# Moving v's casts, loads and border copies in a sparse-attention and MoE kernel

## The chip, the cores and the metric

The kernel runs on one core of one Trainium2 chip. The metric is the time of one execution in microseconds (us). Three runs of the kernel before gave 247.07, 248.79 and 249.06; the median is 248.79.

## What is computed

Four batches, eight heads, 768 tokens, head width 64. Each token attends to the tokens less than 16 away and to 24 block summaries: for every block of 32 tokens the maximum of k and the mean of v. The result, 768 x 512 for each batch, goes through one of eight experts, which is chosen from the mean over the batch's tokens.

```python
k_sum = k.reshape(B, H, nb, block, D).max(axis=3)      # block 32
v_sum = v.reshape(B, H, nb, block, D).mean(axis=3)
mask_l = np.abs(pos[:, None] - pos[None, :]) < window  # window 16
scores_s = scale * einsum(q, k_sum) + np.log(block)
a = softmax(concatenate([where(mask_l, scores_l, -1e9), scores_s]))
attn = a @ concatenate([v, v_sum])
e = argmax(mean_over_tokens(x) @ w_gate)               # one expert for a batch
out = gate * (relu(x @ w1[e]) @ w2[e])
```

## The kernel before, in words

**Attention.** Two heads (a pair) are handled at once, in 12 query blocks of 64. A query block sees 96 keys (its 64 and a border of 16 on either side) and the 24 block summaries, 120 rows in all. The steps of a pair, each a Python function that issues its instructions:

- T (line 190): TensorE transposes k (L194), a copy lays it out in windows as kT (L208 on ScalarE in batch 0, L210 on VectorE later), q likewise (L214, L220), VectorE takes the block maxima kmx (L224), GpSimd copies these behind the windows of kT (L230) and clears kT's spare columns (L233).
- QK (line 238), for one half of the query blocks: scores (L245), exponential on ScalarE (L254), mask on VectorE (L256).
- AV (line 267): attention times v (L278), division (L286, L287).
- X (line 295): transposes to the layout of the MoE (L299, L304), with the sums that the gate needs.

**v.** load_v (line 95) brings one batch's v, eight loads on the SP queue, to v_f in fp32. cast_v (L153; L151 on ScalarE) writes it as bf16 into vblk, of which there are two for alternating batches. halo_v (L157, L158) copies the 16 border rows of each query block from its neighbours, by two DMAs inside SBUF. vsum (line 160) forms the block sums on TensorE (L166, 24 matmuls for each batch), copies them out (L174) and broadcasts them into rows 96 to 119 of vblk, by two DMAs on SP (L178). AV reads vblk after all of these.

**MoE.** gate (line 337) finds the expert, and GpSimd issues the loads of its weights (L362, L367), 4 MB in fp32 that arrive as bf16. h (L396, eviction L403 on ScalarE) and o (L410, L418) are the two layers; they write to three PSUM buffers, the tile hps, in turn. vsum and gate take theirs from the same three.

**Order.** The order of the work on each engine is the order in which the Python code issues it; every engine and every DMA queue works its list off in order. Batch 0's attention runs alone, the beginning of batch 1's too (the first LEAD = 14 of its 30 steps). From then on the MoE of batch b runs with the rest of the attention of b+1 and the beginning of b+2's between its groups; the last batch's MoE runs alone. The steps of batch b also prepare v of batch b+1: four casts on GpSimd, two heads each; in halo, first the loads of v for batch b+2, then the border copies; in vs, the sums. q and k are loaded from the GpSimd queue (L90), two heads at a time for batch 0, all of them at the start, and four at a time for later batches. SP also carries the output stores (L419).

Of the kernel before, what the change touches and what calls it, by code (L numbers as in the profile page):

```python
# [22 lines left out]
def kernel(  # L23
# [36 lines left out]
    kt_pool = ctx.enter_context(tc.tile_pool(name="kt", bufs=3))  # L60
    at_pool = ctx.enter_context(tc.tile_pool(name="at", bufs=3))
    xs_pool = ctx.enter_context(tc.tile_pool(name="xs", bufs=3))
# [14 lines left out]
    vblks = [  # L77
        const_pool.tile([128, NJ + 2, H, D + 1], BF16, name=f"vblk{i}") for i in range(2)
    ]
    kps = kps_pool.tile([128, G, SP + 4], BF16, name="kps")  # L80
    qk_nat = {}
# [13 lines left out]
    def load_v(b):  # L95
        for h in range(H):
            nc.sync.dma_start(
                v_f[16:80, :, h, :], v[b, h].rearrange("(j p) d -> p j d", p=QB)
            )

    load_qk(0, 0, 2)
    load_v(0)
    wg_sb = const_pool.tile([128, NDT, E], FP32, name="wg_sb")
# [4 lines left out]
    nc.scalar.activation(warm, warm, ACT.Exp)  # L108

    for pr in range(1, NP):  # L110
        load_qk(0, 2 * pr, 2 * pr + 2)

    identb = const_pool.tile([128, 128], BF16, name="identb")
    make_identity(nc, identb)

    nc.vector.memset(kps.rearrange("p g c -> p (g c)").bitcast(FP32), 0.0)
    nc.vector.memset(v_f[0:16], 0.0)
    for vb in vblks:
        nc.vector.memset(vb[0:KW, 0, :, :], 0.0)
        nc.vector.memset(vb[0:KW, NJ + 1, :, :], 0.0)  # L120
        nc.vector.memset(vb[0:KW, 1 : NJ + 1, :, D : D + 1], 1.0)

    ones_row = const_pool.tile([1, 128], FP32, name="ones_row")
    nc.vector.memset(ones_row, 1.0)

    mask = const_pool.tile([NR, G, QB // G], BF16, name="mask")
    bind = const_pool.tile([80, NJ, 32], BF16, name="bind")
    it_u = const_pool.tile([KW, G, QB // G], I32, name="it_u")
    m2 = const_pool.tile([KW, G, QB // G], BF16, name="m2")
    nc.gpsimd.iota(it_u, pattern=[[-1, G], [-G, QB // G]], base=0, channel_multiplier=1)  # L130
    nc.vector.tensor_scalar(out=mask[0:KW], in0=it_u, scalar1=1, scalar2=None, op0=ALU.is_ge)
    nc.vector.tensor_scalar(out=m2, in0=it_u, scalar1=31, scalar2=None, op0=ALU.is_le)
    nc.vector.tensor_tensor(out=mask[0:KW], in0=mask[0:KW], in1=m2, op=ALU.mult)
    nc.vector.memset(mask[KW:NR], 1.0)

    it_b = const_pool.tile([80, NJ, 32], I32, name="it_b")
    it_p = const_pool.tile([80, NJ, 32], I32, name="it_p")
    b2 = const_pool.tile([80, NJ, 32], BF16, name="b2")
    nc.gpsimd.iota(it_b, pattern=[[QB, NJ], [-BLK, 32]], base=-16, channel_multiplier=1)
    nc.gpsimd.iota(it_p, pattern=[[0, NJ], [0, 32]], base=0, channel_multiplier=1)  # L140
    nc.vector.tensor_scalar(out=bind, in0=it_b, scalar1=0, scalar2=None, op0=ALU.is_ge)
    nc.vector.tensor_scalar(out=b2, in0=it_b, scalar1=BLK - 1, scalar2=None, op0=ALU.is_le)
    nc.vector.tensor_tensor(out=bind, in0=bind, in1=b2, op=ALU.mult)
    nc.vector.tensor_scalar(out=b2, in0=it_p, scalar1=16, scalar2=None, op0=ALU.is_ge)
    nc.vector.tensor_tensor(out=bind, in0=bind, in1=b2, op=ALU.mult)

    def cast_v(b, h0, h1, eng):
        dst = vblks[b % 2][0:80, 1 : NJ + 1, h0:h1, 0:D]
        src = v_f[:, :, h0:h1, :]
        if eng is nc.scalar:  # L150
            nc.scalar.activation(dst, src, ACT.Copy)  # L151
        else:
            eng.tensor_copy(dst, src)  # L153

    def halo_v(b, h0, h1):
        vb = vblks[b % 2]
        nc.sync.dma_start(vb[0:16, 1 : NJ + 1, h0:h1, :], vb[64:80, 0:NJ, h0:h1, :])  # L157
        nc.sync.dma_start(vb[80:96, 1 : NJ + 1, h0:h1, :], vb[16:32, 2 : NJ + 2, h0:h1, :])  # L158

    def vsum(b):  # L160
        vb = vblks[b % 2]
        vs_ps = mps_pool.tile([128, 512], FP32, name="hps", tag="mps")
        HW = H // 2
        for j in range(NJ):
            for hg in range(2):
                nc.tensor.matmul(  # L166
                    vs_ps[32 * hg : 32 * hg + 32, 0 : HW * (D + 1)],
                    lhsT=bind[:, j, :],
                    rhs=vb[0:80, 1 + j, hg * HW : (hg + 1) * HW, :],
                    start=(j == 0),  # L170
                    stop=(j == NJ - 1),
                )
        vsb = sm_pool.tile([64, HW, D + 1], BF16, name="vsb")
        nc.vector.tensor_copy(  # L174
            vsb, vs_ps[0:64, 0 : HW * (D + 1)].rearrange("p (h c) -> p h c", c=D + 1)
        )
        for hg in range(2):
            nc.sync.dma_start(  # L178
                vb[KW:NR, 1 : NJ + 1, hg * HW : (hg + 1) * HW, :],
                vsb[32 * hg : 32 * hg + NB].unsqueeze(1).to_broadcast([NB, NJ, HW, D + 1]),  # L180
            )

    def attn_steps(b):
# [6 lines left out]
        def T(pr):  # L190
            def f():
                for g in range(G):
                    for hh in range(2):
# [4 lines left out]
                        )  # L198
                kT = kt_pool.tile([128, NJ, 128], BF16, name="kT")
                full = kps[:, :, :]  # L200
# [11 lines left out]
                for g in range(G):  # L212
# [16 lines left out]
                )  # L229
                nc.gpsimd.tensor_copy(  # L230
                    kT[:, :, KW:NR], kmx.unsqueeze(1).to_broadcast([128, NJ, NB])
                )
                nc.gpsimd.memset(kT[:, :, NR:128], 0.0)  # L233
                qTs[pr], kTs[pr] = qT, kT
# [3 lines left out]
        def QK(pr, hf):  # L238
            def f():
                sc = sc_pool.tile([128, 2, 512], FP32, name="sc")  # L240
                for jj in range(NH):
                    j = hf * NH + jj
                    for hh in range(2):
                        rs = slice(hh * D, (hh + 1) * D)
                        nc.tensor.matmul(  # L245
                            sc[:, hh, jj * QB : (jj + 1) * QB],
                            lhsT=kTs[pr][rs, j, :],
                            rhs=qTs[pr][rs, j, :],
                            start=True,
                            stop=True,  # L250
                            tile_position=(hh * D, 0),
                        )
                aT = at_pool.tile([128, 2, NH * QB], BF16, name="aT")
                nc.scalar.activation(aT, sc[:, :, 0 : NH * QB], ACT.Exp, scale=SCALE)  # L254
                a3 = aT[0:NR].rearrange("p h (j c) -> p (h j) c", c=QB)
                nc.vector.tensor_tensor(  # L256
                    out=a3,
                    in0=a3,
                    in1=mask.rearrange("p g e -> p (g e)")
                    .unsqueeze(1)  # L260
                    .to_broadcast([NR, 2 * NH, QB]),
                    op=ALU.mult,
                )
                aTs[pr, hf] = aT
            return f

        def AV(pr, hf):
            def f():
                aT = aTs.pop((pr, hf))
                NS = NH // 2  # L270
                ops_raw = ops_pool.tile([128, 512], FP32, name="ops")
                ops = ops_raw[:, 0 : 2 * NS * (D + 1)].rearrange(
                    "p (h s c) -> p h s c", h=2, c=D + 1
                )
                for hh in range(2):
                    for jj in range(NH):
# [3 lines left out]
                            lhsT=aT[0:NR, hh, jj * QB : (jj + 1) * QB],  # L280
                            rhs=vb[0:NR, 1 + j, 2 * pr + hh, :],
                            start=True,
# [31 lines left out]
        def cast(h0):  # L314
            def f():
                if nxt < B:
                    cast_v(nxt, h0, h0 + 2, nc.gpsimd)
            return f

        def halo():  # L320
            if nxt < B:
                if nxt + 1 < B:
                    load_v(nxt + 1)
                halo_v(nxt, 0, H)

        def vs():
            if nxt < B:
                vsum(nxt)

        steps = [  # L330
            T(0), QK(0, 0), T(1), QK(0, 1), AV(0, 0), QK(1, 0), AV(0, 1), T(2),
            QK(1, 1), AV(1, 0), cast(0), X(0), QK(2, 0), AV(1, 1), cast(2), T(3), QK(2, 1), AV(2, 0),
            cast(4), X(1), QK(3, 0), AV(2, 1), cast(6), QK(3, 1), halo, AV(3, 0), X(2), vs, AV(3, 1), X(3),
        ]
        return steps, xT, pooled
# [93 lines left out]

    cast_v(0, 0, 4, nc.vector)  # L430
    cast_v(0, 4, 8, nc.scalar)
    halo_v(0, 0, H)
    load_v(1)
    steps0, xT0, pooled0 = attn_steps(0)
    steps0[0]()
    vsum(0)
    load_qk(1, 0, 4)
    for s in steps0[1:]:
        s()
    moe = moe_groups(0, xT0, *gate(0, pooled0))  # L440
    load_qk(1, 4, 8)

    LEAD = 14
    queue = []
# [14 lines left out]
    pend = []  # L459
    load_qk(2, 0, 4)  # L460
    load_qk(2, 4, 8)
    start_attn(1)
# [43 lines left out]
```

## Time and profile before

| what | us |
|---|---|
| median of three runs | 248.79 |
| the profiled execution, its own time | 248.07 |
| its span, first to last instruction | 246.4 |
| busy: TensorE / VectorE / ScalarE / GpSimd | 154.6 / 99.3 / 92.8 / 50.6 |
| SP's eight loads of batch 0's v, first issue to last | 0.86 to 15.96 |
| border copies of batch 1, 2, 3: first issue | 60.43, 107.84, 156.06 |
| sums of batch 0, 1, 2, 3: first matmul | 26.82, 66.34, 115.30, 160.12 |
| weight loads of the four batches: first issue | 74.40, 124.12, 168.95, 209.62 |
| first MoE matmul; first of the last batch | 97.39; 218.72 |

In a row of the timeline stand the start, the duration, the engine, the line, the operation, what it writes and reads, how many instructions are merged, and in brackets how long the engine had been idle and who released it. In a row of the waits stand the total, how often, and the longest. In a row of a window stand its length, the busy time (and number of instructions) of TensorE, its weight loads, VectorE, ScalarE and GpSimd, the granted clock of TensorE, the DMA engines' busy share and GB/s. In the slices each digit is the busy share of a fortieth of the span, in tenths.

### The profile page before, as it was taken

Reading aid. Unit: us, or ns where it says so; the run is one execution under the profiler, and the core shown is the slowest. Engines: PE = TensorE matmul, PEld = TensorE weight load, DVE = VectorE, ACT = ScalarE, POOL = GpSimd, SP = SyncE. Lnnn points to the kernel's source line nnn. Section 1 sums busy time; section 2 is a strip of 40 time slices with the busy share of each in tenths; the row PEclk is TensorE's granted clock in tenths of the full one; section 3 lists DMA queues with packets and bytes.
Section 4 is the critical chain, followed back from the end, with each engine's and each line's share of the span. In section 5 each row is a group of like instructions: output and inputs, shape, how many; then the busy total and the mean of one; then the engine's idle time right before and its main releaser. Section 6 shows DMA issues by size and latency. Waiting matters only on the chain. (4 is left out here: it accounts for less than half of the span.)

```text
span 246.4 us, 4656 instructions
## 1 busy us (share of the span) xinstructions
PE 154.6 (63%) x1939; PEld 92.9 (38%) x1960; DVE 99.3 (40%) x192; ACT 92.8 (38%) x167; POOL 50.6 (21%) x82
## 2 busy tenths in 40 slices
PE   0200610764252427997779999587699995449993
PEld 0200510653132325654335565243366542125541
DVE  6851040587034547842247883215683542000000
ACT  2006130454120214484415668321467745115532
POOL 7300210055009215320071235003110100200000
PEclk9999999999999999999979999997999999558998
DMA  6993999047717999693479990534990032792033
GB/s 111 205 194 35 145 177 138 8 87 131 109 49 115 189 204 206 144 145 52 94 139 199 242 223 13 119 105 97 182 212 3 1 130 85 115 225 48 0 128 128
DMA packets 45013, 30.38 MB, mean 123 GB/s; under 512 B 26688, under 2 KB 40256, under 8 KB 44864
## 3 DMA queue, kind: packets, MB, share of 16 engines
q0 software_dynamic: 13264, 14.68, 37.3%
q1 hardware_dynamic: 31728, 15.40, 30.3%
q8 instruction: 15, 0.25, 0.4%
q14 instruction: 6, 0.05, 0.1%
HBM read 35.67 MB, written 6.29 MB: 170 GB/s over the span
## 5 line engine op out<-in xcount | busy, mean ns | idle before, releaser
L396 PE MATMUL hps<-xT_b,w_sb 128*128 128x256 bf16 (+1 forms) x246 | 49.4, 343 | 7.4 <-DMA w_sb<-in_moe_w_dram 6.6
L410 PE MATMUL hps<-w_sb,hT_sb 128*128 128x512 bf16 x181 | 46.8, 403 | 1.3 <-issue 1.0
L254 ACT ACTIVATE aT<-sc 128x768 bf16<-128x768 f32 x32 | 25.9, 808 | 42.8 <-PE sc L245 42.8
L403 ACT ACTIVATE hT_sb<-hps 128x512 bf16<-128x512 f32 x64 | 29.9, 491 | 25.9 <-PE hps L396 25.6
L256 DVE TENSOR_TENSOR aT<-aT,mask 120x768 bf16<-120x768 bf16 x32 | 23.6, 736 | 36.4 <-ACT aT L254 36.4
L418 ACT ACTIVATE o_sb<-hps,gcol 128x512 f32<-128x512 f32 x24 | 16.5, 687 | 43.4 <-PE hps L410 32.6
L396 PEld LDWEIGHTS <-w_sb 128*128 128x128 bf16 x256 | 24.0, 102 | 23.2 <-DMA w_sb<-in_moe_w_dram 7.5
L230 POOL COPY kT<-kmx 128x288 bf16<-128x288 bf16 x16 | 9.2, 574 | 93.1 <-DVE kmx L224 86.3
L410 PEld LDWEIGHTS <-hT_sb 128*128 128x128 bf16 x192 | 18.1, 101 | 21.1 <-issue 3.8
L166 PE MATMUL hps<-vblk,bind 80*32 80x260 bf16 x96 | 8.6, 348 | 27.1 <-DMA vblk<-vblk 27.1
L278 PE MATMUL ops<-vblk,aT 120*64 120x65 bf16 x384 | 14.1, 217 | 16.3 <-DMA vblk<-vsb 12.6
L245 PE MATMUL sc<-qT,kT 64*128 64x64 bf16 x384 | 13.1, 210 | 14.6 <-POOL kT L233 13.7
L278 PEld LDWEIGHTS <-aT 120*64 120x64 bf16 x384 | 10.3, 126 | 23.7 <-issue 16.3
L304 ACT ACTIVATE xT_b<-tps 128x768 bf16<-128x768 bf16 x16 | 12.9, 808 | 16.1 <-PE tps L299 16.1
L210 DVE COPY kT<-kps 128x1152 bf16<-128x1152 bf16 x12 | 16.2, 1353 | 5.3 <-PE kps L194 4.1
L287 DVE TENSOR_TENSOR xs<-ops,rv 128x384 bf16<-128x384 f32 x32 | 17.8, 557 | 1.1
L245 PEld LDWEIGHTS <-kT 64*128 64x128 bf16 x384 | 9.0, 105 | 23.9 <-POOL kT L233 17.6
L224 DVE TENSOR_REDUCE kmx<-kT 128x24 bf16<-128x768 bf16 x16 | 15.1, 944 | 7.3 <-ACT kT L208 7.3
L153 POOL CAST vblk<-v_f 80x1536 bf16<-80x1536 f32 x12 | 17.7, 1505 | 0.0
L194 PE MATMUL kps<-identb,k_nat 96*64 96x96 bf16 x256 | 11.0, 244 | 10.3 <-POOL identb masks.py:199 7.2
L362 POOL DMA_DIRECT2D w_sb<-in_moe_w_dram x5 | 3.8, 755 | 66.2 <-DVE gcol L386 50.6
L166 PEld LDWEIGHTS <-bind 80*32 80x32 bf16 x96 | 6.1, 119 | 28.9 <-issue 22.8
(56 smaller groups left out, 120.4 us busy)
## 6 DMA issues: line engine op xcount, KB each, us to landing
w_sb<-in_moe_w_dram POOLq DMA_DIRECT2D x7, 1024.0 KB, 13.2
v_f<-in_v_dram SPq DMA_DIRECT2D x32, 192.0 KB, 5.3
out_dram<-o_sb SPq DMA_DIRECT2D x24, 256.0 KB, 2.6
k_nat<-in_k_dram POOLq DMA_DIRECT2D x6, 384.0 KB, 17.5
q_nat<-in_q_dram POOLq DMA_DIRECT2D x6, 384.0 KB, 18.7
vblk<-vblk SPq DMA_DIRECT2D x8, 195.0 KB, 5.9
vblk<-vsb SPq DMA_DIRECT2D x8, 146.2 KB
w_sb<-in_moe_w_dram POOLq DMA_DIRECT2D x2, 512.0 KB, 6.2
```

What stands on the lines that cost most here:

```text
L153: eng.tensor_copy(dst, src)
L210: nc.vector.tensor_copy(kdst, win)
L224: nc.vector.tensor_reduce(out=kmx.rearrange("p (j n) -> p j n", n=2), in_=kT[:, :, 16:80].rearrange("p j (n w) -> p j n w", w=BLK), axis=AX.X,
L245: nc.tensor.matmul(sc[:, hh, jj * QB : (jj + 1) * QB], lhsT=kTs[pr][rs, j, :], rhs=qTs[pr][rs, j, :], start=True, stop=True, tile_position ...
L254: nc.scalar.activation(aT, sc[:, :, 0 : NH * QB], ACT.Exp, scale=SCALE)
L256: nc.vector.tensor_tensor(out=a3, in0=a3, in1=mask.rearrange("p g e -> p (g e)") .unsqueeze(1) .to_broadcast([NR, 2 * NH, QB]), op=ALU.mult,)
L278: nc.tensor.matmul(ops[(j % 2) * QB : (j % 2 + 1) * QB, hh, jj // 2, :], lhsT=aT[0:NR, hh, jj * QB : (jj + 1) * QB], rhs=vb[0:NR, 1 + j, 2 ...
L287: nc.vector.tensor_tensor(out=xss[pr][:, hf * NS : (hf + 1) * NS, :, :].rearrange("p s h d -> p h s d"), in0=ops[:, :, :, 0:D], in1=rv.uns ...
L396: nc.tensor.matmul(hps[:, 0 : c1 - c0], lhsT=w1_sb[:, dt, ft * 128 : (ft + 1) * 128], rhs=xT_b[:, dt, c0:c1], start=(dt == 0), stop=(dt == ...
L403: nc.scalar.activation(hT[:, ft, c0:c1], hps[:, 0 : c1 - c0], ACT.Relu)
L410: nc.tensor.matmul(o_ps, lhsT=hT[:, ft, st * 128 : (st + 1) * 128], rhs=w2_sb[:, ft, :], start=(ft == 0), stop=(ft == NFT - 1),)
L418: nc.scalar.activation(o_sb, o_ps, ACT.Copy, scale=gcol[:, 0:1])
```

## The change

- Batch 0's v is loaded with its border rows above (80 rows of v_f instead of 64), so that one of its two border copies goes. Only the first pair's q and k are loaded ahead of it. GpSimd then copies single elements (tok) of heads 3 and 6, which makes it wait for their v, before it issues the loads of pair 1 and of pairs 2 and 3.
- Batch 0's v is handled in two halves of four heads (v0), between the attention steps: cast on VectorE or ScalarE, border copy, sums, broadcast; then batch 1's loads of v.
- The casts of later batches go from GpSimd to VectorE. Batch 1's last three casts, its border copies and its sums come after batch 0's gate.
- Later loads of v are issued in vs, after the broadcast of the sums. In batches 1 and 2 halo comes one step earlier.
- The copy of kmx into kT goes from GpSimd to ScalarE; the clearing of kT's spare columns is done once, for three fixed kT tiles.
- vblk loses its two empty border blocks; the mask now depends on the query block. Masks are made by affine_select on GpSimd instead of iota and comparisons. at_pool has 5 buffers instead of 3, AV of batch 0 writes to the hps buffers, LEAD is 11 instead of 14.

```diff
     def load_v(b):
         for h in range(H):
+            if b > 0:
+                nc.sync.dma_start(v_f[16:80, :, h, :], v[b, h].rearrange("(j p) d -> p j d", p=QB))
+                continue
+            j0 = 1 if h == 0 else 0
             nc.sync.dma_start(
-                v_f[16:80, :, h, :], v[b, h].rearrange("(j p) d -> p j d", p=QB)
+                v_f[:, j0:NJ, h, :],
+                bass.AP(tensor=v.tensor, offset=v.offset + (h * S + j0 * QB - 16) * D,
+                        ap=[[D, 80], [QB * D, NJ - j0], [1, D]]),
             )
+            if h == 0:
+                nc.sync.dma_start(v_f[16:80, 0, 0, :], v[0, 0, 0:QB, :])
...
-    for pr in range(1, NP):
-        load_qk(0, 2 * pr, 2 * pr + 2)
...
-    nc.vector.memset(v_f[0:16], 0.0)
...
+    keep(mask1, [[-1, G], [-G, QB // G]], -1, 1)
+    keep(mask1, [[1, G], [G, QB // G]], 31, -1)
+    keep(row_in, [[0, 1]], 79, -1)
+    keep(bind, [[QB, NJ], [-BLK, 32]], -16, 1)
+    keep(bind, [[-QB, NJ], [BLK, 32]], 47, -1)
+    keep(bind, [[0, NJ], [0, 32]], -16, 1)
+    tok = const_pool.tile([80, 2], BF16, name="tok")
+    nc.gpsimd.tensor_copy(tok[:, 0:1], v_f[:, NJ - 1, 3, 0:1])
+    load_qk(0, 2, 4)
+    nc.gpsimd.tensor_copy(tok[:, 1:2], v_f[:, NJ - 1, 6, 0:1])
+    load_qk(0, 4, 6)
+    load_qk(0, 6, 8)
...
+    for t in kts:
+        nc.gpsimd.memset(t[:, :, NR:128], 0.0)
...
     def halo_v(b, h0, h1):
         vb = vblks[b % 2]
-        nc.sync.dma_start(vb[0:16, 1 : NJ + 1, h0:h1, :], vb[64:80, 0:NJ, h0:h1, :])
-        nc.sync.dma_start(vb[80:96, 1 : NJ + 1, h0:h1, :], vb[16:32, 2 : NJ + 2, h0:h1, :])
+        if b > 0:
+            nc.sync.dma_start(vb[0:16, 1:NJ, h0:h1, :], vb[64:80, 0 : NJ - 1, h0:h1, :])
+        nc.sync.dma_start(vb[80:96, 0 : NJ - 1, h0:h1, :], vb[16:32, 1:NJ, h0:h1, :])
...
-                nc.gpsimd.tensor_copy(
-                    kT[:, :, KW:NR], kmx.unsqueeze(1).to_broadcast([128, NJ, NB])
-                )
-                nc.gpsimd.memset(kT[:, :, NR:128], 0.0)
+                nc.scalar.activation(
+                    kT[:, :, KW:NR], kmx.unsqueeze(1).to_broadcast([128, NJ, NB]), ACT.Copy
+                )
...
-                    cast_v(nxt, h0, h0 + 2, nc.gpsimd)
+                    cast_v(nxt, h0, h0 + 2, nc.vector)
...
         def halo():
             if nxt < B:
-                if nxt + 1 < B:
-                    load_v(nxt + 1)
                 halo_v(nxt, 0, H)
         def vs():
             if nxt < B:
-                vsum(nxt)
+                vsum(nxt, (0, 1))
+                if nxt + 1 < B:
+                    load_v(nxt + 1)
+        def v0(hg):
+            def f():
+                cast_v(0, 4 * hg, 4 * hg + 4, (nc.vector, nc.scalar)[hg])
+                halo_v(0, 4 * hg, 4 * hg + 4)
+                vsum(0, (hg,))
+                if hg == 1:
+                    init_vblk(1)
+                    load_v(1)
+            return f
+        if b == 0:
+            steps = [
+                T(0), QK(0, 0), QK(0, 1), v0(0), T(1), QK(1, 0), QK(1, 1), AV(0, 0), v0(1), AV(0, 1),
+                T(2), AV(1, 0), X(0), QK(2, 0), AV(1, 1), QK(2, 1), T(3), X(1), AV(2, 0), QK(3, 0),
+                AV(2, 1), QK(3, 1), X(2), AV(3, 0), cast(0), AV(3, 1), X(3), cast(2), cast(4), cast(6), halo, vs,
+            ]
...
-    cast_v(0, 0, 4, nc.vector)
-    cast_v(0, 4, 8, nc.scalar)
-    halo_v(0, 0, H)
-    load_v(1)
     steps0, xT0, pooled0 = attn_steps(0)
-    steps0[0]()
-    vsum(0)
+    for s in steps0[:-5]:
+        s()
     load_qk(1, 0, 4)
-    for s in steps0[1:]:
-        s()
     moe = moe_groups(0, xT0, *gate(0, pooled0))
     load_qk(1, 4, 8)
-    LEAD = 14
+    load_qk(2, 0, 4)
+    load_qk(2, 4, 8)
+    for s in steps0[-5:]:
+        s()
+    LEAD = 11
```

## The prediction

> **What bounds the kernel now.** I read the page's slices first, then the waits up to 97 us, then the timeline at those waits, then the busy time of 97.4 to 209.6 us.
>
> ```profile
> PE   0200610764252427997779999587699995449993
> DMA  6993999047717999693479990534990032792033
> ```
>
> A slice is 6.16 us. TensorE is nearly empty for its first 16 slices (97 us), full with holes to slice 33, and then alone with the last batch's MoE. The waits in those 97 us (total, times, longest):
>
> ```profile
> PE hps L166 <- DMA vblk<-vblk: 22.4, 2, 17.6
> PE ops L278 <- DMA vblk<-vsb: 12.6, 1, 12.6
> PE sc L245 <- POOL kT L233: 11.0, 5, 5.9
> PE kps L194 <- DMA k_nat<-in_k_dram: 3.1, 1, 3.1
> ```
>
> All are about v, or about GpSimd being busy. The timeline places them (start, duration):
>
> ```profile
> 19.78 2.78 ACT L151 ACTIVATE vblk<-v_f 80x3072 bf16<-80x3072 f32 x1 [17.41 <-DMA v_f<-in_v_dram]
> 23.85 14.19 SPq L97 DMA_DIRECT2D v_f<-in_v_dram  x8
> 29.53 0.50 PE L245 MATMUL sc<-qT,kT 64*128 64x64 bf16 x12
> 38.14 1.93 SPq L178 DMA_DIRECT2D vblk<-vsb  x2
> 44.48 0.54 PE L278 MATMUL ops<-vblk,aT 120*64 120x65 bf16 x12 [12.59 <-DMA vblk<-vsb]
> 60.43 0.65 SPq L157 DMA_DIRECT2D vblk<-vblk  x1
> 66.34 2.78 PE L166 MATMUL hps<-vblk,bind 80*32 80x260 bf16 x24 [4.80 <-DMA vblk<-vblk]
> 74.40 1.50 POOL L362 DMA_DIRECT2D w_sb<-in_moe_w_dram  x2 [15.31 <-DVE gcol L386]
> 80.75 0.49 POOL L230 COPY kT<-kmx 128x288 bf16<-128x288 bf16 x1
> 81.41 0.50 PE L245 MATMUL sc<-qT,kT 64*128 64x64 bf16 x12 [5.88 <-POOL kT L233]
> 90.96 0.85 PE L194 MATMUL kps<-identb,k_nat 96*64 96x96 bf16 x16 [3.06 <-DMA k_nat<-in_k_dram]
> 97.39 1.49 PE L396 MATMUL hps<-xT_b,w_sb 128*128 128x512 bf16 x3 [0.33 <-issue]
> ```
>
> First scores at 29.53, after v has been loaded, cast, copied and summed. The block sums' broadcast is ready near 30 but stands on SP behind the next batch's v loads until 38.14, and TensorE waits to 44.48. The weight load leaves at 74.40, the first MoE matmul at 97.39. From there:
>
> ```profile
> 97.40:209.60 112.20, 96.00 (x1210) 54.48 (x1228) 55.73 (x112) 57.02 (x113) 22.48 (x34) 0.97 0.62 122
> ```
>
> TensorE is 86% busy (96.0 of 112.2), VectorE and ScalarE half. So nearly all of what this change can win lies before 97.4, and MoE 0 to 2 is where it can lose.
>
> **Part A, start to first scores (now 29.53).** The 80-row loads move 80/64 of 1.57 MB, 1.97 MB, with the first q/k pair (0.39 MB, as written) beside them. Pair 1 follows when head 3 has landed, the others after head 6: then 7/8 of v and two pairs have passed, 1.72 + 0.79 = 2.51 MB. DMA moved 195 to 234 GB/s in the full stretches of 6 to 16 us, and 150 in 36 to 38 us with v nearly alone. At 200, from 2.2 us on, head 6 is in at 14.8, visible about 15.3. GpSimd then issues four loads (0.66 each, L90) and only then sets the spare kT columns (0.18), which the scores read: 18.3. I take 19.0, with 18.3 and 22 (at 150 GB/s) as ends. T(0) is long done: q and k were there at 8.3, and identb comes earlier, behind two DMA issues instead of eight. The new selects on GpSimd cost at most 3 x 0.88 (0.29 for 128 columns in make_identity, times three) plus about 0.5; VectorE's 5.18 us memset of v_f goes. Both are covered by the wait for v. Gain 10.5.
>
> **Part B, first scores to weight issue (now 44.9).** Two score steps (2 x (0.50 + 0.81) plus hand-overs and a mask) end at 22.4; cast of four heads 1.76; half the sums 1.4 (12 of the 24 matmuls in 2.78); 25.6. The sums no longer wait for border rows in batch 0. Their broadcast leaves at 26 and lands by about 30 (4.4 after the issue ended, as at 40.07 to 44.45). T(1), its copies and two score steps take until 32.0, which covers it. ScalarE's cast, 2.78, then stands open: 34.8, sums 36.3, AV 36.8. From T(2) to the weight issue it is now 74.40 - 46.19 = 28.2; out go the wait of 4.80 and the sums of 2.78, in comes a cast of two heads, 0.88 (half of 1.76, VectorE's row): 21.5. Weight issue at 58.3, gain 16.1. On SP, border copy (0.59) and broadcast (0.85) of each half now pass ahead of batch 1's eight v loads, which lose nothing that anybody waits for. The next batch's q/k half now leaves at once after the start's loads, and its v leaves SP at 37, so v is in by 50.
>
> **Part C, weight issue to first MoE matmul (now 23.0).** Here the change adds to the path: the other three casts, border copies and sums of batch 1 now follow the gate. Casts 2.65 less the 0.25 by which the gate's last copy precedes the issue, 2.4; border copies 5.9 (4.1 to 7.4 to landing, L157); sums 2.8; T(0) with its chain 0.85 + 1.36 + 1.3 and ScalarE's copy 0.41 (between 0.38 for 256 columns and 0.60 for 512), with hand-overs 4.3: scores at 15.4, against 7.0 now. GpSimd's six DMA issues no longer stand before them. To the second AV step it was 6.5, now about 7.4, since the exponentials queue on ScalarE behind T(1)'s copy; T(2), scores and AV 2.7. In all 25.5. The second q/k half lands 16.6 after the weight issue, as now (74.40 to 90.96), and T(2) comes at 22.8: its 3.06 wait goes. MoE starts at 83.8: gain 13.6. Batch 2's v, queued behind the broadcast from 71 on, shares the queues with q/k; first needed about 86, 15 us later.
>
> **Part D, MoE 0 to 2 (now 112.2).** Three lead steps move in: 0.50 + 0.35 + 0.38 = 1.2 at the faster rate seen after 102 us. Border copies issued one step earlier: waits of 1.85 and 2.80 shrink to about 0.5 and 1.5, -2.6. Score waits on GpSimd (1.14 and 1.56) shrink by 1.5. Masks stretched by GpSimd's casts become short, off the path; VectorE takes eight casts of 0.88 for batches 2 and 3, 7.0 us on an engine with half its time free, where one stands just ahead of a kT copy (inside the 1.2 below). Against this, the kmx copy on ScalarE:
>
> ```profile
> 51.55 1.79 DVE L256 TENSOR_TENSOR aT<-aT,mask 120x768 bf16<-120x768 bf16 x1 [1.14 <-ACT aT L254]
> 99.88 1.35 DVE L210 COPY kT<-kps 128x1152 bf16<-128x1152 bf16 x1
> 101.14 0.55 DVE L220 COPY qT<-tps 128x768 bf16<-128x768 bf16 x1
> 101.61 0.94 DVE L224 TENSOR_REDUCE kmx<-kT 128x24 bf16<-128x768 bf16 x1
> 102.71 0.42 POOL L230 COPY kT<-kmx 128x288 bf16<-128x288 bf16 x1 [3.85 <-DVE kmx L224]
> ```
>
> Between the start of the kT copy and the end of kmx lie 2.67 us in which ScalarE now waits, and behind it the MoE evictions that free the three PSUM buffers. Three steps of the first MoE half hide about 1.5, so about 1.2 stays open for each of the four T steps there; the five among output groups (1.7 us of TensorE each) are hidden. Ends 0 and 9 x 2.67 = 24; I take 4.8, the nearer to the row of three buffers. On SP batch 3's v loads (8 x 0.65 = 5.2 of issue; 10.27 for the eight at 97.48, which waited for GpSimd's casts) now stand behind the sums' broadcast and ahead of the output stores. Behind them wait the o_sb buffers, three, of which one is filled every 3 us around the gate: 9 us of cover, so nothing; without it up to 5. Net 1.2 - 2.6 - 1.5 + 4.8 = +1.9.
>
> **Sum.** 13.6 - 1.9 = 11.7 off the span, the tail (209.62 to 246.4, a 9 us weight wait and MoE 3) unchanged. 246.4 - 11.7 = 234.7; with the 1.67 around the span 236.4, against the profiled run's 248.07. The median, 248.79, lies 0.72 above that run: 237.
>
> [...] In the row at 51.55 a mask took 1.79 beside GpSimd's cast, and 0.55 alone. [...] For the kmx copy the rows give 0.41 on ScalarE and 0.57 on GpSimd. [...]
>
> **Rivals.**
> - ScalarE becomes the bound (slower). All nine T steps pay 2.67: +19 on the sum, 256. It decides from 1.8 per step on (16.5 / 9, where 16.5 is the sum's gain without the holes). For it: ScalarE is 7.3 of 10 us busy at 137 to 147. Against: it is 51% busy over the stage, and three buffers lie between.
> - Given back after the gate. The border copies, alone with weights in the queues, land only when weights and second q/k half have passed (18.4 after the issue, q's 92.85): sums 10.1 later, 247. For it: 7.4 was the longest, in mixed traffic. Against: one 11 KB packet for each partition, sharing each queue.
> - Holes covered, copies at 4.1: 237 - 4.8 - 1.8 = 230.
> - The first part does not do what it says: v at 150 GB/s keeps the tokens, and so the kT memset and the scores, until 22: 240.
>
> **Chances and range.** Likeliest case 0.64 (232 to 242), holes covered 0.12, slow v 0.08, given back 0.08, ScalarE bound 0.08. A measurement can tell about 1%: 246.3 and 251.3. Faster by more: 0.64 + 0.12 + 0.08 and 0.03 of the give-back, 0.87; same 0.05; slower 0.08. The range 229 to 246 leaves out the ScalarE case and most of the give-back, 0.13, and a little below.
>
> **What would show it.** First scores near 19, their wait on GpSimd's kT memset; no wait for vsb's broadcast over 3; weight issue near 58; sums of batch 1 waiting some 6 for the border copies; no k_nat wait at T(2); MoE from 84; evictions of the first MoE half late behind the kmx copy, TensorE idle about 1 after such T steps. Wrong if scores start past 22, if the weight issue comes after 62, or if MoE 0 to 2 takes over 118 or under 110.

## The result, and the profile after

The changed kernel takes 257.55 us (median of four runs, 255.14 to 258.88) against 247.93 of the kernel before beside it: ratio 1.0375, 95% interval 1.028 to 1.047. It is slower, where 237 and faster were forecast. Here and below a time is the median of all executions, while a ratio leaves out those in a slower state that some executions fall into. The profiled execution took 257.47, its span is 255.9. Line numbers of the changed kernel are those of the diff's new file: v_f loads L100 and L105, casts L184 and L186, border copies L191 and L192, block sums L200, their broadcast L213, kmx copy L266, scores L280, exponentials L289, weights L417 and L422, MoE matmuls L451 and L465, evictions L458 and L473, stores L474.

The page's slices, now 6.40 us each:

```profile
PE   0205457731254889967550498964989897539993
DMA  7999209708999980469999400446950023495033
```

The early part is denser, but inside the MoE the 22nd slice (134 to 141 us) is 0, between a 5 and a 4. TensorE's waits in MoE 0 to 2 name it (total, times, longest):

```profile
PE hps L451 <- ACT o_sb L473: 12.6, 1, 12.6
...
PE sc L280 <- ACT kT L266: 4.0, 2, 2.9
...
PE hps L200 <- DMA vblk<-vblk: 0.5, 1, 0.5
```

Up to the MoE the timeline reads as the prediction has it, with two steps longer than thought, the half sums of batch 0 (22.88) and the border copies before the sums of batch 1 (69.06):

```profile
17.81 0.50 PE L280 MATMUL sc<-qT,kT 64*128 64x64 bf16 x12 [8.42 <-POOL kT L178]
...
22.88 2.76 PE L200 MATMUL hps<-vblk,bind 80*32 80x260 bf16 x12 [3.16 <-DVE vblk L186]
...
57.08 2.28 POOL L417 DMA_DIRECT2D w_sb<-in_moe_w_dram  x2 [37.81 <-DVE grec L435]
...
69.06 2.57 PE L200 MATMUL hps<-vblk,bind 80*32 80x260 bf16 x22 [8.51 <-DMA vblk<-vblk]
...
85.91 1.22 PE L451 MATMUL hps<-xT_b,w_sb 128*128 128x512 bf16 x3 [0.33 <-issue]
```

The second half sum, at 34.66, takes 2.76 too; batch 1's border copies leave at 60.15. The first MoE matmul starts at 85.91, against 97.39: here the changed kernel is 11.5 us ahead. The window of MoE 0 to 2 shows where it loses more than that (length; busy TensorE, weight loads, VectorE, ScalarE, GpSimd; clock; DMA share; GB/s):

```profile
85.91:219.50 133.59, 99.98 (x1239) 56.90 (x1259) 61.81 (x125) 61.63 (x126) 5.97 (x9) 0.91 0.57 112
```

MoE 0 to 2 take 133.6 instead of 112.2 (forecast: 114.1; over 118 was named as a sign of being wrong), with TensorE busy for only 4 us more. The tail, 219.50 to 255.9, takes 36.4 (36.8 before). The timeline around the hole:

```profile
111.41 14.05 SPq L100 DMA_DIRECT2D v_f<-in_v_dram  x8
...
114.58 0.75 POOL L417 DMA_DIRECT2D w_sb<-in_moe_w_dram  x1 [49.98 <-DVE grec L435]
...
125.56 18.51 SPq L474 DMA_DIRECT2D out_dram<-o_sb  x4
...
143.03 0.69 ACT L473 ACTIVATE o_sb<-hps,gcol 128x512 f32<-128x512 f32 x1 [17.29 <-DMA out_dram<-o_sb]
...
143.77 0.59 PE L451 MATMUL hps<-xT_b,w_sb 128*128 128x512 bf16 x1 [12.55 <-ACT o_sb L473]
```

SP issues batch 3's v at 111.41, behind the broadcast. Three microseconds later GpSimd issues the weights of MoE 1 and then q and k. From MoE 0's third store on, the stores follow v on SP. None of these lands before ScalarE, out of o_sb buffers, has waited 17.29; its evictions free no PSUM buffer; TensorE waits 12.55. Of the DMA issues of 111 to 146 us (KB each, median us from issue to landing) this row shows why:

```profile
v_f<-in_v_dram SPq DMA_DIRECT2D x8, 192.0 KB, 13.0
```

and the same of the kernel before, 97 to 125 us:

```profile
v_f<-in_v_dram SPq DMA_DIRECT2D x8, 192.0 KB, 4.2
out_dram<-o_sb SPq DMA_DIRECT2D x2, 256.0 KB, 3.5
```

These medians are over the few loads whose landing the trace tells, here the fifth of eight alone. The packets in the trace tell of all eight. Before, v went ahead of the weights, nearly alone in the engines: its last packet moved at 113.3, 15.8 after the first issue and 11 before the weights left. Now the last one moves at 141.9, 30.5 after the first issue, and the first packet of a store behind v on SP at 140.1. From 126 to 140 us SP's queue moved 2189 packets and GpSimd's (weights, q, k) 2188, one for one, but v's are of 256 B and GpSimd's mostly of 1 KB: 0.55 MB against 2.18.

### The profile page after: what moved, and what is told of

It is laid out like the page before. It is cut to its first block, busy times and chain, and to the rows that moved or that the text cites. A ratio compares the mean times of both kernels' runs of the same rounds, so it can differ in the third digit from the quotient of the medians.

```text
span 255.9 us, 4606 instructions
## 1 busy us (share of the span) xinstructions
PE 160.2 (63%) x1936; PEld 95.8 (37%) x1960; DVE 99.1 (39%) x201; ACT 97.2 (38%) x183; POOL 25.5 (10%) x46
## 5 line engine op out<-in xcount | busy, mean ns | idle before, releaser
L451 PE MATMUL hps<-xT_b,w_sb 128*128 128x256 bf16 (+1 forms) x245 | 51.8, 348 | 22.6 <-ACT o_sb L473 12.6
L465 PE MATMUL hps<-w_sb,hT_sb 128*128 128x512 bf16 x179 | 46.5, 404 | 1.9 <-issue 1.2
L290 DVE TENSOR_TENSOR aT<-aT,mask 120x768 bf16<-120x768 bf16 x32 | 17.8, 558 | 64.5 <-ACT aT L289 64.4
L451 PEld LDWEIGHTS <-w_sb 128*128 128x128 bf16 x256 | 24.2, 104 | 39.5 <-issue 20.9
L458 ACT ACTIVATE hT_sb<-hps 128x512 bf16<-128x512 f32 x64 | 29.3, 497 | 16.8 <-PE hps L451 16.8
L473 ACT ACTIVATE o_sb<-hps,gcol 128x512 f32<-128x512 f32 x24 | 16.5, 686 | 44.2 <-PE hps L465 19.4
L289 ACT ACTIVATE aT<-sc 128x768 bf16<-128x768 f32 x32 | 25.9, 810 | 12.7 <-PE sc L280 12.7
L280 PE MATMUL sc<-qT,kT 64*128 64x64 bf16 x384 | 13.5, 212 | 25.3 <-ACT kT L266 9.4
L266 ACT ACTIVATE kT<-kmx 128x288 bf16<-128x288 bf16 x16 | 7.1, 442 | 56.3 <-DVE kmx L260 56.3
L465 PEld LDWEIGHTS <-hT_sb 128*128 128x128 bf16 x192 | 18.7, 102 | 22.0 <-issue 4.8
L200 PE MATMUL hps<-vblk,bind 80*32 80x260 bf16 x96 | 12.0, 347 | 18.1 <-DMA vblk<-vblk 9.0
L417 POOL DMA_DIRECT2D w_sb<-in_moe_w_dram x5 | 4.5, 911 | 186.7 <-DVE gcol L441 98.9
L280 PEld LDWEIGHTS <-kT 64*128 64x128 bf16 x384 | 9.7, 107 | 33.9 <-issue 14.3
L200 PEld LDWEIGHTS <-bind 80*32 80x32 bf16 x96 | 7.6, 118 | 21.7 <-issue 18.5
L325 DVE TENSOR_TENSOR xs<-ops,rv 128x384 bf16<-128x384 f32 x24 | 13.4, 557 | 0.8
L186 DVE CAST vblk<-v_f 80x1536 bf16<-80x1536 f32 (+1 forms) x13 | 13.4, 1042 | 0.5 <-DMA v_f<-in_v_dram 0.5
L337 PE MATMUL tps<-identb,xs 128*128 128x128 bf16 x96 | 10.3, 247 | 4.6 <-DVE xs L325 3.2
```

The source lines that it names most:

```text
L200: nc.tensor.matmul(vs_ps[32 * i : 32 * i + 32, 0 : HW * (D + 1)], lhsT=bind[:, j, :], rhs=vb[0:80, j, hg * HW : (hg + 1) * HW, :], start=( ...
L280: nc.tensor.matmul(sc[:, hh, jj * QB : (jj + 1) * QB], lhsT=kTs[pr][rs, j, :], rhs=qTs[pr][rs, j, :], start=True, stop=True, tile_position ...
L290: nc.vector.tensor_tensor(out=aT[0:NR], in0=aT[0:NR], in1=mask[:, hf * NH : (hf + 1) * NH, :] .rearrange("p j c -> p (j c)") .unsqueeze(1) ...
L451: nc.tensor.matmul(hps[:, 0 : c1 - c0], lhsT=w1_sb[:, dt, ft * 128 : (ft + 1) * 128], rhs=xT_b[:, dt, c0:c1], start=(dt == 0), stop=(dt == ...
L458: nc.scalar.activation(hT[:, ft, c0:c1], hps[:, 0 : c1 - c0], ACT.Relu)
L465: nc.tensor.matmul(o_ps, lhsT=hT[:, ft, st * 128 : (st + 1) * 128], rhs=w2_sb[:, ft, :], start=(ft == 0), stop=(ft == NFT - 1),)
```

## The experiments

The queue theory: the stall of the stores is the loss. The rival: ScalarE's copy of kmx, in front of the evictions, is. The medians of before beside the runs were 248.5 to 249.1; "D" is the stretch from the first MoE matmul to the fourth weight issue in the profiled execution (112.2 before, 133.6 after).

**1. v ahead of the border copies again.**

```diff
 def halo():
+    if b > 0 and nxt + 1 < B: load_v(nxt + 1)
     halo_v(nxt, 0, H)
 def vs():
     vsum(nxt, (0, 1))
-    if nxt + 1 < B: load_v(nxt + 1)
+    if b == 0 and nxt + 1 < B: load_v(nxt + 1)
```

> The changed kernel, but batch 3's eight v loads are issued ahead of batch 2's border copies again, as in the kernel before, so ahead of the second weight load. Queue theory (the output stores stand on SP behind v loads that share the DMA engines with weights and q/k): the 17.3 us wait of o_sb for its store and TensorE's 12.6 behind it go, and with them the 13.65 us at clock 0.5 that follow (half of it lost, 6.8): 257.5 - 19.4 = 238, between 236 and 243. ScalarE theory (the kmx copy in front of the evictions costs the 21 us): no change, 255 to 259.

Measured: 244.83, ratio to before 0.983 (0.974 to 0.992); D 122.7. ScalarE no longer waits for a store. The last packet of v moves at 106.3, before the weights leave at 115.77, and the first of the stores of 84 to 116 us, the only one whose landing is told, lands in 4.2:

```profile
out_dram<-o_sb SPq DMA_DIRECT2D x3, 256.0 KB, 4.2
```

**2. Six output buffers.** `o_pool`: bufs=3 becomes bufs=6.

> The changed kernel with six o_sb buffers instead of three; the order of every queue stays. Queue theory: the stores still land only after the v loads (about 143 us), but ScalarE no longer waits for them, so TensorE's 12.6 and the slow clock behind it go: 238 to 243. If instead the traffic itself (weights, q/k and v at once) holds TensorE through late weights or late k, the waits move to those and 250 or more is left. ScalarE theory: 255 to 259.

Measured: 244.50, 0.980 (0.973 to 0.987); D 121.0. v is as late as ever (its last packet moves at 141.1), and so are the stores behind it on SP, but nobody waits for them:

```profile
124.61 23.64 SPq L474 DMA_DIRECT2D out_dram<-o_sb  x5
```

Two different cures win the same 13, so the stall is shown. Both end 6.5 above the 238 of the queue theory and 1.5 to 1.8 above the top of its ranges: something else was left.

**3. Stores on ScalarE's queue.** In L474 `nc.sync` becomes `nc.scalar`.

> The changed kernel with the 24 output stores issued from ScalarE's queue instead of SP's; the v loads stay late and meet the weights as before. Order theory (a store waits for all v packets that stand ahead of it in the same queue): stores land in 3 to 8 us beside the other traffic and the stall goes, 238 to 244, with up to some us lost to ScalarE's issuing (24 issues of about 0.6, most of them beside idle time). Bandwidth theory (the engines are full, so a store is late on any queue): the waits of o_sb stay near 17 and the time near 257.

Measured: 248.29, 1.003 (0.997 to 1.008); D 124.7. The time is above the 238 to 244 of the order theory, but the rest is as it says. The v loads still meet the weights (last packet at 143.4), the stores now pass them (109 to 146 us), and ScalarE, with three buffers, waits for no store:

```profile
v_f<-in_v_dram SPq DMA_DIRECT2D x8, 192.0 KB, 4.9
out_dram<-o_sb ACTq DMA_DIRECT2D x4, 256.0 KB, 6.0
```

The 4.9 is of two v loads that left before the weights. The 6.0 is of one store, issued at 129.47; of the two before it, issued at 117.98 and 123.44, the last packets end 6.4 and 5.8 later. So it is about 6 instead of 17 or more, in engines as full as before (181 GB/s over these 37 us, 180 in experiment 2): the place in the queue did it, not the bandwidth. The 4 above experiment 2 may come from the 24 issues of 0.34 us each on ScalarE; no run tested that.

**4. kmx copy back on GpSimd.** In L266 `nc.scalar.activation` becomes `nc.gpsimd.tensor_copy`.

> The changed kernel with the copy of the block maxima into kT back on GpSimd, its only other change undone being that the spare columns stay zeroed once at the start. ScalarE theory: the 21 us in MoE 0 to 2 are holes before the evictions, so 236 to 245. Queue theory: the stall stays; the waits of evictions shrink by about 3 us, but scores wait for GpSimd at its DMA issues (1 to 6 each time in the kernel before): 253 to 260.

Measured: 252.80, 1.019 (1.008 to 1.029); D 130.0. The stall stays (TensorE waits 10.96 for o_sb), so the rival is not the cause of the 21; but 4.7 are won, a little more than the queue theory allowed.

**5. That move alone, in the kernel before.** load_v for batch 3 goes from halo to behind vsum; nothing else of the change.

> The kernel before, with one thing of the change alone: batch 3's eight v loads leave SP behind batch 2's border copies, sums and broadcast, instead of ahead of the border copies. Queue theory: the same stall as in the changed kernel (12.6 us of TensorE and some of the slow clock behind it), which undoing cost 12.7 and 13.0 there: 248.7 + 9 to 14 = 258 to 263. If the stall needs the change's other parts (its earlier loads, the idle GpSimd): no change, 247 to 251.

Measured: 264.38, 1.064 (1.054 to 1.075): 15.9 slower, beyond even the expectation. The same chain, with the weights leaving at 122.01 and ScalarE waiting 18.66 for a store:

```profile
116.98 12.71 SPq L97 DMA_DIRECT2D v_f<-in_v_dram  x8
...
129.80 26.16 SPq L421 DMA_DIRECT2D out_dram<-o_sb  x6
...
146.85 0.69 ACT L420 ACTIVATE o_sb<-hps,gcol 128x512 f32<-128x512 f32 x1 [18.66 <-DMA out_dram<-o_sb]
...
148.29 0.50 PE L245 MATMUL sc<-qT,kT 64*128 64x64 bf16 x12 [14.35 <-ACT aT L254]
```

One of the change's moves, by itself, costs more than the whole change lost (15.9 against 9.6).

**6. kT zeroed first** (with six buffers, as in 7 to 11). The three memsets of L178 go ahead of the tok copies.

> Six o_sb buffers, and the spare columns of the three kT are zeroed on GpSimd ahead of the two token copies instead of behind them and their loads. If the first scores wait only for that: scores at 11.5 instead of 17.3 to 17.8, and the whole span 5 to 6 shorter than with six buffers alone (244.5): 238 to 240. If v or the later q/k pairs then bound batch 0 (the second half's v lands near 15.5, the pairs behind it): the scores start early, the weight issue moves by less than 2, and 242 to 245 is left.

Measured: 239.92, 0.965 (0.957 to 0.973). The time is the first theory's, the path lies between the two: scores start at 12.09 (17.26 in experiment 2), but the weight issue is only 3.4 earlier and the MoE 2.2, since batch 0 then waits 4.9 for a broadcast.

**7. kmx copy on VectorE.** In L266 `nc.scalar.activation` becomes `nc.vector.tensor_copy`.

> Six o_sb buffers, and the copy of the block maxima into kT on VectorE, straight behind the maxima themselves, instead of on ScalarE. If ScalarE's wait for the maxima holds back evictions and exponentials by the 4.8 us of the prediction, 239 to 241 against 244.5 with six buffers alone; the waits of scores for ScalarE's kT copy (8.3 in total) and of MoE matmuls for evictions (3.7) shrink. If these holes are covered or VectorE pays for them: 243 to 246.

Measured: 236.64, 0.953 (0.944 to 0.961): 7.9 less than experiment 2, and below what either theory allowed. The window of D, experiment 2 and then this one:

```profile
84.13:205.08 120.95, 102.39 (x1264) 56.89 (x1261) 62.30 (x126) 61.44 (x126) 5.98 (x8) 0.94 0.65 124
```

```profile
83.41:196.15 112.74, 95.73 (x1239) 55.19 (x1259) 63.65 (x135) 59.01 (x116) 5.98 (x9) 0.97 0.70 136
```

D is 8.2 shorter. Of TensorE's waits in it, those for evictions and exponentials in experiment 2 are gone from the list of experiment 7:

```profile
PE hps L451 <- ACT hT_sb L458: 3.7, 6, 1.1
PE sc L280 <- ACT aT L289: 3.2, 2, 2.9
```

The waits of scores for the copy itself did not shrink, as the expectation had it; first experiment 2, then 7:

```profile
PE sc L280 <- ACT kT L266: 2.9, 1, 2.9
```

```profile
PE sc L280 <- DVE kT L266: 4.8, 3, 2.7
```

The copy takes 235 ns on VectorE, 442 on ScalarE; ScalarE had waited 58.5 us in all for kmx, with everything behind it. How the 8.2 divides between these waits and the rest is not shown, but that the copy's place makes it is: D is 120.1 to 121.0 in the four runs with six buffers and the copy on ScalarE (2, 6, 8 and 9) and 112.4 to 113.9 in the three with it on VectorE (7, 10 and 11). D is now that of the kernel before.

**8. Half sums in two groups of output rows.** Each half sum: 24 matmuls of two heads, alternating between rows 0 to 31 and 32 to 63, instead of 12 of four heads.

> Six o_sb buffers, and each of batch 0's two half sums as 24 matmuls of two heads (130 columns) that alternate between two groups of 32 output rows, instead of 12 matmuls of four heads (260 columns) into one group. A half sum took 2.76 us in the changed kernel, as long as the full sum of 24 matmuls in two groups (2.78). If matmuls into two groups run side by side and those into one do not, a half sum now takes 1.4 to 1.6 and the weight issue comes 2.4 earlier than 56.5. If 2.8 is a price of 24 matmuls or of the cold start, whatever their width, it stays 2.6 or more.

Measured, a single run: 240.89; the weight issue is at 54.24, 2.3 earlier.

```profile
22.72 1.48 PE L223 MATMUL hps<-vblk,bind 80*32 80x130 bf16 x24 [3.16 <-DVE vblk L186]
```

The same columns in 1.48 instead of 2.76, as the expectation has it if two groups run side by side and one does not.

**9. q and k behind the border copies.** After the first gate GpSimd copies one border element before it issues q and k.

> Six o_sb buffers, and behind the first gate GpSimd reads one border row of batch 1 (a token) before it issues the six q/k loads, so the border copies share the engines with the weights alone. In the changed kernel the border copies were issued at 60.15 and the sums resumed at 69.06, 8.9 later, with weights and q/k in the queues; with six buffers 59.6 to 67.69, 8.1. If q/k's packets stretch them: 5 to 6.5 from issue to sums, and the first MoE matmul 1.5 to 3 earlier than 27.6 behind the weight issue, unless T(2) then waits for k. If the weights alone stretch them: 8 or more, and nothing won.

Measured, a single run: 242.28. A miss: border copies from 59.73, sums at 67.52, 7.8 later (8.1 without the token), MoE at 84.36, 27.7 behind the weight issue. q and k hardly stretch them.

```profile
67.52 2.57 PE L200 MATMUL hps<-vblk,bind 80*32 80x260 bf16 x22 [7.38 <-DMA vblk<-vblk]
...
68.16 0.69 POOL L92 DMA_DIRECT2D k_nat<-in_k_dram  x1 [0.34 <-issue]
```

What is left beside them is the weights (4 MB); that these alone stretch them fits, but no run took them away.

**10 and 11. All mends together** (2, 6, 7 and 8), and with the token of 9.

> The changed kernel with the four mends together: six o_sb buffers, the kT columns zeroed first, the block maxima copied on VectorE, the half sums in two groups. If each price was separate: 244.5 less 7.9 (VectorE), 4.6 (zeroed first) and 2.3 to 3.6 (two groups): 228 to 230. If batch 0 is then bound by v and q/k landing, so that the two in batch 0 overlap: 231 to 234.

> The four together, and the token of the run before last ahead of the q/k loads. If the border copies are stretched by q/k: 1.5 to 3 less than the four alone. If T(2) or the next batches then wait for k instead: no gain, or a loss of 1 to 3.

Measured: 225.85, 0.907 (0.900 to 0.914), and 224.53, 0.901 (0.892 to 0.910). Between the two no difference can be told. Both are some 10% faster than the kernel before, more than the separate prices promised; in 10 scores start at 11.32, weights leave at 47.67, the MoE starts at 74.86, D is 113.9.

**12. kmx on VectorE, three output buffers.** The edit of 7 alone.

> The changed kernel with its three o_sb buffers, and only the copy of the block maxima moved to VectorE: the stall stays, the other price goes. If the two prices are separate, the stall costs here what it cost beside the copy on ScalarE (257.5 - 244.5 = 13.0), and the run takes 257.5 - 7.9 = 249.6, 248 to 252, with MoE 0 to 2 in 112.7 + 12.6 = 125.3. If the copy's holes lay partly inside the stall: 252 to 256. If a faster ScalarE only reaches the full buffers sooner, so that the stall grows by what the copy gave: 255 to 259.

Measured: 252.48, 1.013 (1.004 to 1.022), just above the 248 to 252 of separate prices. The trace shows that ScalarE, no longer held up by the copy, reaches the full buffers sooner and waits longer:

```profile
139.72 0.69 ACT L473 ACTIVATE o_sb<-hps,gcol 128x512 f32<-128x512 f32 x1 [19.82 <-DMA out_dram<-o_sb]
140.45 0.58 PE L451 MATMUL hps<-xT_b,w_sb 128*128 128x512 bf16 x1 [16.05 <-ACT o_sb L473]
```

The wait of TensorE grew from 12.55 to 16.05. So, by the medians, the stall costs 13.0 beside the copy on ScalarE (after against 2) and 15.8 without it (12 against 7; 15.9 in 5); the copy costs 7.9 without the stall (2 against 7) and 5.1 beside it (after against 12). That the two overlap rests on the traces (D is 130.2 here, 17.5 above experiment 7, where it is 12.6 between after and 2): each ratio is good to 2 us or so, and by the ratios the stall costs about 14 and 15, the copy 7 and 6. Together the two cost 257.55 - 236.64 = 20.9, which is nearly all that D lost.

## Why the prediction was wrong, point by point

- **Part A, right.** Scores at 17.8 (19.0 forecast, 18.3 the early end), waiting for GpSimd's kT memset as said, and no more than that: experiment 6 moves them to 12.
- **Part B, right in sum, wrong in a term.** 39.3 from scores to weight issue, as forecast, since errors cancel; that is luck. Each half sum took 2.76, not 1.4: "12 of the 24 matmuls in 2.78" took half of a row in which the matmuls alternated between two groups (experiment 8). T(2) to the weight issue took 19.4, not 21.5.
- **Part C, mis-sized by 3.3.** 28.8, not 25.5: border copies 8.9 to the sums, not 5.9. The rival that they land 18.4 later did not come true, nor is q/k what delays them (experiment 9). T(2) did not wait for k, as forecast.
- **Part D, the failed step.** "9 us of cover, so nothing; without it up to 5" priced batch 3's v loads ahead of the stores by their issue, 5.2 us. What held the stores was the transfer ahead of them in the queue, not the issue: beside weights, q and k the issuing of v took 14 us, and its last packet moved 30.5 after the first issue. The cover was no worse than thought: evictions filled the three buffers at 112.4, 118.0 and 123.0, some 5 apart, and the next output group was ready at 128.1, 17 after v's first issue; the first store behind v landed at 143. Six buffers hold out until the stores land (experiment 2). The move costs 13 to 16, by experiments 1, 2, 5 and 12. The prediction did ask what v meets in the engines, for batch 2's v, and stopped there; for batch 3's it counted SP alone, and no rival had the stores in it.
- **Part D, mis-sized.** The kmx copy: 4.8 taken, between 0 and 24; 7.9 measured without the stall. The working looked at PSUM evictions alone; TensorE did wait for them as forecast (3.0 in all in the changed kernel, 1.2 at most), but the exponentials behind the copy waited too (3.2 in experiment 2), and the rest is open. The clock of the stage does not divide by it: 0.94 to 0.96 with the copy on ScalarE and six buffers, 0.93 to 0.97 with it on VectorE. The shrinking of the border waits came true (4.6 to 0.5), that of the score waits did not: 2.7 for GpSimd before, 4.0 for ScalarE after.
- **The rival "ScalarE becomes the bound"** ended near the measured time, 256, by another mechanism. It added 19, and D did lose 21, but only 5 to 8 of that is the copy's. A time that fits is no proof of its cause: experiments 2 and 4 had to tell them apart.
- **What VectorE took on.** With the kmx copy on VectorE experiment 7 won 7.9, where the prediction had 4.8 open for the copy on ScalarE; the copy's own time, 442 against 235 ns, makes 3.3 over all 16. Of the casts one row tells something: the two weight issues at 57.08, beside them, took 2.28, against 1.50 before. No run took the casts away from there, and no wait of TensorE for weights or k followed up to the end of MoE 2 (219.50).

## What to carry to other kernels

When a load is moved later on a queue, price it by when its last byte lands in the traffic it will then meet, and ask which stores stand behind it on that queue and how many output buffers cover them. A share of a row's time is only a price if what made the row fast (here 24 matmuls alternating between two groups, 1.48, where 12 into one took 2.76) is still there in the share. An instruction that waits for another engine, put on an engine that frees buffers, brings its wait along: in MoE 0 to 2 ScalarE stood 28.0 us before nine copies of 0.44 each, and the evictions and exponentials behind them stood too.

## What was not expected of the hardware

- **The queue decided, at the same traffic.** Behind v on SP a store took over 17 us; on ScalarE's queue, beside the same v and weights, about 6 (experiment 3; 181 GB/s, 180 in experiment 2). What that saved was the wait behind another transfer's packets. In the changed kernel SP's queue and GpSimd's moved 2189 and 2188 packets from 126 to 140 us, and the stores on SP moved only as v ran out: their first packet at 140.1, v's last at 141.9.
- **Half clock, in and after the stall.** There TensorE was granted half its clock (0.51 from 134.8 to 148.4); the rows before and after are two shorter such stretches of the changed kernel (0.52 and 0.51), which began just before idle times of TensorE of 2.63 and 2.92 ended:

```profile
124.40:127.80 3.40, 3.23 (x19) 1.38 (x19) 1.75 (x4) 0.81 (x1) 0.00 (x0) 0.52 1.21 196
134.80:148.40 13.60, 4.41 (x17) 2.26 (x17) 2.09 (x4) 4.36 (x9) 0.00 (x0) 0.51 0.73 162
...
179.20:185.90 6.70, 6.16 (x76) 3.55 (x78) 3.15 (x4) 2.36 (x5) 0.00 (x0) 0.51 1.16 218
```

Work resumed at 143.77; the clock was full again from 148.5, nearly 5 later, so that up to 2.4 more were lost (an estimate: half of that time). In the kernel before the same stage had two stretches at half clock, of 3.4 each, from 125.0 and 169.4.
- **Two groups of output rows took half the time of one.** 24 matmuls of 130 columns, alternating between two groups of 32 rows, took 1.48; 12 of 260 into one group took 2.76 (experiment 8).
